# A two-layer expert stage: the second product in one pass of 512 columns, outputs in rows of 4 KB

## The chip, the cores and the metric

The kernel runs on one core of one Trainium2 chip. The metric is the device time of one execution in microseconds; the median of several executions is compared. The profile comes from one execution, which has its own time.

The core has a matrix engine (TensorE, PE in the profile, with PEld for its weight loads), VectorE (DVE), ScalarE (ACT), GpSimd (POOL) and a queue, SP, which issues all transfers of this kernel. TensorE reads SBUF and writes PSUM; ScalarE and VectorE copy from PSUM to SBUF. Transfers between SBUF and device memory run on 16 DMA engines.

## The reference

Three stages in a row on 2304 tokens of 512 features (4 sequences of 576).

```python
x = attention(q, k, v)                      # 8 heads of 64; 4 local, 4 strided masks
h = x @ w_in                                # 512 -> 2048
x = (h * sigmoid(1.702 * h)) @ w_out        # 2048 -> 512
logits = x @ phi                            # 32 slots: 8 experts of 4
slot_input = softmax_over_tokens(logits).T @ x
for e in range(8):                          # 4 slots of each expert
    slot_out[e] = relu(slot_input[e] @ w1[e]) @ w2[e]   # 512 -> 1024 -> 512
out = softmax_over_slots(logits) @ slot_out # (2304, 32) @ (32, 512)
```

The output is 2304 x 512 in float32, 4.72 MB. The weights w1 and w2 of the experts are 16.8 MB each.

## The kernel before

Most of the span is attention and the 512 to 2048 product, with the token softmax gathered on the way. The change touches only the last part, the experts and the output.

All 32 slots of the 8 experts go through TensorE at once. The 128 rows of a weight tile are 128 values of the inner dimension; a tile of 1 MB holds [128, 4, 512] floats. `load_ex` (L479) asks SP for the next tile; `ex[0]` to `ex[3]` are parts of w_out, `ex[4]` to `ex[19]` belong to the first expert product, `ex[20]` to `ex[35]` to the second. They go into buffers that other work has freed: `e`, `x0`, `x1` and `wi` tiles, and parts of the large tile gT, which `gx_tile` (L474) hands out as four slots of [128, 4, 512] in turn. A load waits on SP until the last user of its buffer is done. Tiles 23 to 35 take buffers of first-product tiles (or of others freed then), and so are issued as that product goes on.

The slot inputs are made at L590 to L598: spp is summed on TensorE, copied to `acc_s` in two halves (VectorE L592, ScalarE L593), multiplied with a selection (sip) and copied to `si`. `expand1(G, n)` (L632) makes the first product for four experts and half of the hidden units: 16 matmuls of 512 columns into one PSUM tile hp. `hidden_t` turns it for the second product.

`expand2(half, n)` (L658, matmul at L667) is the second product. The 512 output columns are cut into blocks of 256, 128 and 128:

```python
COLS = [(0, 256), (256, 128), (384, 128)]
```

On the host (`_layouts`), w2 is laid out so that a tile of 1 MB holds 2 (or 4) of the 16 slices of the inner dimension for the columns of one block, with 4 experts beside one another. So the first block uses tiles 20 to 27, the second 28 to 31, the third 32 to 35. A float32 matmul has two records in the profile. `slot_out(half)` (L669) takes a finished block from PSUM: ScalarE writes one part of `so` (L672), VectorE the other (L673).

The combine weights of the tokens, one number for each token and slot, are split in two parts (`combine_split`, L609), turned by TensorE and copied by ScalarE into cT (`combine_t`, L619, copy at L624), five chunks of 512 tokens (the last of 256). The order of instructions on an engine is set by a planner that follows the program's order by priority and the estimated readiness; in the profile, three of the five L624 copies stand at 386 to 389 us.

`combine(half, k, n)` (L675) makes the output for n groups of 128 tokens and one block of columns: a matmul for each group (L684), copies to one of the four slots of gT, by ScalarE (L687) and VectorE (L689) in turn, and one store (L690). A partition holds one token of each group, so a row of the store is the block's width: 1 KB or 512 B. Blocks 0 and 1 are combined between the `expand2` calls of the following block, the last one at the end:

```python
for half in range(1, len(COLS)):
    todo = list(PARTS)
    tiles = COLS[half][1] // 32
    for n in range(tiles):
        expand2(half, n)
        if n:
            for _ in range(-(-len(todo) // (tiles - n))):
                combine(half - 1, *todo.pop(0))
    slot_out(half)
```

Two other lines serve below for comparison: L241, where ScalarE writes attention outputs into x, contiguous for the local heads and with a step of 32 tokens for the strided ones, and the store of w_out slices to device memory (wo_scr), in rows of 2 KB. L319 is the product with w_in, in fp32r, the type of the combine matmul.

Of the kernel before, what the change touches and what calls it, by code (L numbers as in the profile page):

```python
# [9 lines left out]
F32 = mybir.dt.float32  # L10
# [4 lines left out]
ALU = mybir.AluOpType  # L15
# [4 lines left out]
NT, DM, FF = B * S, 512, 2048  # L20
# [9 lines left out]
CHUNKS = [(0, 512), (512, 512), (1024, 512), (1536, 512), (2048, 256)]  # L30
NF = FF // 128
TFROM = 5
COLS = [(0, 256), (256, 128), (384, 128)]
PARTS = [(0, 2), (2, 4), (6, 4), (10, 4), (14, 4)]
LAST = [(0, 4), (4, 4), (8, 4), (12, 4), (16, 2)]
F64_SMALL = float(np.uint32(897 << 20).view(np.float32))
F64_LARGE = float(np.uint32((1151 << 20) - 1).view(np.float32))
C_ID, C_REP, C_ZC, C_ML, C_ML0, C_MS, C_END = 0, 128, 256, 258, 354, 450, 514
# [3 lines left out]
def tile_kernel(ctx: ExitStack, tc: tile.TileContext, lqk, lv, sqk, sv, wraw, phi, wexp, cst, out):  # L42
    nc = tc.nc
    P = 128
# [4 lines left out]
    xp = ctx.enter_context(tc.tile_pool(name="xp", bufs=3))  # L49
# [15 lines left out]
    def mtile(name):  # L65
        return ps_m.tile([P, 512], F32, tag="m", name=name)
# [19 lines left out]
    zc = cs[:, C_ZC:C_ZC + 2]  # L86
# [263 lines left out]
    side, st, todo = [], {}, []  # L350
# [120 lines left out]
    ex = {}  # L471
    gxn = [0]

    def gx_tile():  # L474
        k = gxn[0] % 4
        gxn[0] += 1
        return gt[0][:, 4 * k:4 * k + 4]
# [95 lines left out]
    c = len(CHUNKS) - 1  # L573
# [14 lines left out]
    for f in range(NF):  # L588
        j = f % 4
# [10 lines left out]
    cT0 = tl.tile([P, 2048], F32R, name="cT0")  # L600
# [3 lines left out]
    def ttile(name):  # L604
        return ps_t.tile([P, 512], F32, tag="t", name=name)
# [3 lines left out]
    def combine_split(c):  # L609
        c0, N = CHUNKS[c]  # L610
        ntt = N // 128
        t = c4t[:, c % 2]
        c4s[c] = t
        c4 = t.rearrange("p (u r e q) -> p u r e q", r=2, e=2, q=8)[:, :4 * ntt]
        cc = ca[:, c0 // 128:c0 // 128 + ntt].rearrange("p t (j q) -> p (t j) q", q=8).unsqueeze(2).to_broadcast([P, 4 * ntt, 2, 8])
        nc.vector.tensor_copy(c4[:, :, :, 0].bitcast(F32R), cc)
        nc.vector.tensor_tensor(c4[:, :, :, 1].bitcast(F32R), cc, c4[:, :, :, 0], op=ALU.subtract)

    def combine_t(c):  # L619
        c0, N = CHUNKS[c]  # L620
        ctp = ttile(f"ctp_{c}")
        for tt in range(N // 128):
            nc.tensor.transpose(ctp[:, 128 * tt:128 * tt + 128], c4s[c][:, 128 * tt:128 * tt + 128], ident)
        nc.scalar.copy(cT0[:, c0:c0 + N] if c < 4 else cT1, ctp[:, :N])  # L624

    hzt = e1p.tile([P, 2, 8, P], F32, tag="e", name="hz")
    hc = e1p.tile([P, 4, 512], F32, tag="e", name="hc")
# [17 lines left out]
    def hidden_t(G, n):  # L645
        hT = mtile(f"hT_{G}_{n}")
        for q in range(4):
            nc.tensor.transpose(hT[:, 128 * q:128 * q + 128], h1[G, n][:, 128 * q:128 * q + 128], ident)
        sv = hT.rearrange("p (q m) -> p q m", m=128)
        dv = hz[G][:, 4 * n:4 * n + 4, :]  # L650
        for j in range(4):
            o = 40 * j + 4 * G
            nc.vector.tensor_copy(dv[:, :, 32 * j:32 * j + 32].rearrange("p f (r q) -> p f r q", q=8)[:, :, :, 4 * G:4 * G + 4],
                                  sv[:, :, o:o + 4].unsqueeze(2).to_broadcast([P, 4, 4, 4]))

    ops, obs = [], {}

    def expand2(half, n):  # L658
        c0, w = COLS[half]
        per = DM // w  # L660
        if n == 0:
            ops.append(mtile(f"op_{half}"))
        t = ex[20 + c0 // 32 + n].rearrange("p j f -> p (j f)").rearrange("p (k j f) -> p k j f", k=per, j=4)
        for k in range(per):
            G, fc = (per * n + k) // 8, (per * n + k) % 8
            for j in range(4):
                nc.tensor.matmul(ops[half][32 * j:32 * j + 32, :w], hz[G][:, fc, 32 * j:32 * j + 32], t[:, k, j], start=G + fc == 0, stop=G + fc == 8)  # L667

    def slot_out(half):  # L669
        c0, w = COLS[half]  # L670
        o = ops[half][:, :w]
        nc.scalar.mul(so[:, 0, c0:c0 + w], o, zc[:, 0:1])  # L672
        nc.vector.scalar_tensor_tensor(so[:, 1, c0:c0 + w], o, zc[:, 1:2], so[:, 0, c0:c0 + w].bitcast(F32), op0=ALU.mult, op1=ALU.add)  # L673

    def combine(half, k, n):  # L675
        c0, w = COLS[half]
        per = DM // w
        ob = gx_tile().rearrange("p a b -> p (a b)")[:, :n * w].rearrange("p (t f) -> p t f", f=w)
        for a in range(0, n, per):
            z = min(n, a + per)  # L680
            fp = ttile(f"fp_{half}_{k}_{a}")[:, :w * (z - a)].rearrange("p (t f) -> p t f", f=w)
            for t in range(a, z):
                tok = P * (k + t)
                nc.tensor.matmul(fp[:, t - a], cT0[:, tok:tok + P] if k + t < 16 else cT1[:, tok - 2048:tok - 2048 + P], so[:, 1, c0:c0 + w], start=True, stop=True)  # L684
            obs[0] = not obs.get(0)
            if obs[0]:
                nc.scalar.copy(ob[:, a:z], fp)  # L687
            else:
                nc.vector.tensor_copy(ob[:, a:z], fp)  # L689
        nc.sync.dma_start(out[P * k:P * (k + n), c0:c0 + w].rearrange("(t p) f -> p t f", p=P), ob)  # L690

    expand1(0, 0)
    hz = [hzt[:, 0], hzt[:, 1]]
# [11 lines left out]
    for c in range(2):  # L705
        combine_split(c)
        combine_t(c)
# [9 lines left out]
    fin = e1p.tile([P, 4, 512], F32R, tag="e", name="fin")  # L717
    so, cT1 = fin[:, :2], fin[:, 2, :256]
    hidden_t(1, 0)
    for n in range(8):  # L720
        expand2(0, n)
        if n == 2:
            hidden_t(1, 1)
        if n >= 5:
            combine_split(n - 3)
            combine_t(n - 3)
    slot_out(0)
    for half in range(1, len(COLS)):
        todo = list(PARTS)
        tiles = COLS[half][1] // 32  # L730
        for n in range(tiles):
            expand2(half, n)
            if n:
                for _ in range(-(-len(todo) // (tiles - n))):
                    combine(half - 1, *todo.pop(0))
        slot_out(half)
    for k, n in LAST:
        combine(len(COLS) - 1, k, n)


def _layouts(q, k, v, w_in, w_out, phi, w1, w2):
# [63 lines left out]
```

## Time and profile before

| | us |
|---|---|
| timed runs, median (lowest, highest) | 441.59 (441.43, 441.65) |
| profiled execution | 442.75 |
| its span (first to last instruction) | 441.0 |
| busy: TensorE / VectorE / ScalarE / GpSimd | 410.5 / 264.9 / 195.3 / 78.5 |
| DMA | 80.90 MB, mean 183 GB/s |

A line of the profile names the source line, engine and operation, the tile written and the tiles read, the shape and a count. Starts are counted from the span's start. In brackets stands how long the engine was idle before, and what released it. The granted clock is TensorE's: 1.00 is 2.4 GHz, 0.50 is 1.2 GHz. Busy time of a matmul includes its way through the pipeline, so neighbouring records overlap. DMA share is the mean busy share of the 16 DMA engines; packets may overlap, so it can pass 1.

### The profile page before, as it was taken

How to read it: one execution, taken by the hardware profiler on the slowest of the kernel's cores; microseconds unless marked ns; L12 is line 12 of the kernel's file. 1: busy time of each engine (PE TensorE's matmuls, PEld its weight loads, DVE VectorE, ACT ScalarE, POOL GpSimd, SP SyncE). 2: the span in 40 equal slices, each digit the busy share in tenths (PEclk: the TensorE clock that was granted, in tenths of full speed). 3: DMA queues.
4: the chain of work that ended last, by engine and by line, in shares of the span. 5: the costliest groups of instructions: out<-in, count | busy, mean ns of one | idle time of the engine just before them, and what ended most of it. 6: DMA issues, size and time to landing. Idle time of an engine off the chain costs nothing.

```text
span 441.0 us, 10075 instructions
## 1 busy us (share of the span) xinstructions
PE 410.5 (93%) x4082; PEld 282.8 (64%) x4088; DVE 264.9 (60%) x564; ACT 195.3 (44%) x639; POOL 78.5 (18%) x96
## 2 busy tenths in 40 slices
PE   8877898998989999999999999999999998999965
PEld 4555675655556767777676776776777795244654
DVE  2689999998987454565466535546454654431212
ACT  2785777766674644454543355321212222020312
POOL 0354445645540110100100001000000000000000
PEclk9999999999999999999999999999999999899995
DMA  8956757585663030221411101870003799779998
GB/s 245 358 164 221 248 177 278 182 310 180 223 199 113 9 100 2 91 81 52 153 42 58 38 2 36 283 289 1 1 0 143 291 387 349 271 305 424 426 355 251
DMA packets 25614, 80.90 MB, mean 183 GB/s; under 512 B 2144, under 2 KB 9440, under 8 KB 21472
## 3 DMA queue, kind: packets, MB, share of 16 engines
q1 hardware_dynamic: 25568, 80.26, 51.3%
q8 instruction: 32, 0.52, 0.5%
q14 instruction: 14, 0.11, 0.1%
HBM read 71.34 MB, written 8.91 MB: 182 GB/s over the span
## 4 chain that ended last, share of the span: by engine, by line
PE 67%; DVE 15%; ACT 6%; DMA 4%; POOL 4%; issue 3%; ACTq 0%; POOLq 0%
PE h L319 37%; PE u L433 5%; DMA out<-gT 4%; DVE wc L262 4%; PE lg L338 4%; PE s L161 3%; PE hp L637 3%; ACT ts L179 3%; DVE wc L263 3%; PE op L667 2%; PE ptp L197 2%; DVE wc L261 2%; PE av L216 2%; POOL wc L260 2%; PE busy L78 2%
## 5 line engine op out<-in xcount | busy, mean ns | idle before, releaser
L319 PE MATMUL h<-x,wi 128*128 128x512 f32 (+1 forms) x960 | 222.3, 379 | 1.2 <-DVE x L242 1.1
L319 PEld LDWEIGHTS h<-x,wi 128*128 128x128 f32 x960 | 161.8, 189 | 47.1 <-issue 13.8
L323 DVE SCALAR_TENSOR_TENSOR gT<-gT,h 128x512 f32<-128x512 f32 (+1 forms) x64 | 40.6, 634 | 62.2 <-ACT gT L322 61.6
L322 ACT ACTIVATE gT<-h 128x512 f32<-128x512 f32 (+1 forms) x64 | 35.5, 555 | 69.3 <-PE h L319 69.0
L179 ACT ACTIVATE ts<-ts,nmx 128x64 f32<-128x64 f32 (+1 forms) x120 | 41.6, 348 | 29.2 <-DVE nmx L174 28.9
L182 POOL TENSOR_TENSOR ts<-ts,sm 128x384 f32<-128x384 f32 (+2 forms) x32 | 28.6, 894 | 138.9 <-DVE sm L181 74.9
L346 DVE STREAM_TRANSPOSE gT<-gT 128x512 f32<-128x512 f32 (+1 forms) x64 | 41.0, 648 | 0.8
L260 POOL TENSOR_SCALAR wc<-wc 128x512 f32<-128x512 f32 x32 | 24.2, 759 | 29.1 <-ACT wc L259 29.1
L262 DVE SCALAR_TENSOR_TENSOR wc<-raw,wc 128x512 uint32<-128x512 uint32 x32 | 26.8, 839 | 0.3
L263 DVE SCALAR_TENSOR_TENSOR wc<-raw,wc 128x512 uint32<-128x512 uint32 x32 | 26.7, 835 | 0.2
L338 PE MATMUL lg<-gT,wp 128*32 128x512 f32 (+1 forms) x128 | 25.6, 564 | 0.7 <-ACT wp L295 0.6
L271 POOL TENSOR_TENSOR wi<-wc,wi 128x512 fp32r<-128x512 f32 x16 | 23.0, 1436 | 14.1 <-ACT wi L270 14.1
L197 PE MATMUL ptp<-cs,ts 128*96 128x128 f32 (+1 forms) x120 | 17.7, 280 | 8.4 <-POOL ts L182 7.7
L161 PE MATMUL s<-qk 64*64 64x96 f32 (+1 forms) x552 | 25.0, 236 | 0.2 <-DMA qk<-lqk 0.2
L161 PEld LDWEIGHTS s<-qk 64*64 64x64 f32 x552 | 20.9, 134 | 6.4 <-issue 4.9
L180 DVE TENSOR_SCALAR sm<-sm 128x5 f32<-128x5 f32 (+2 forms) x32 | 8.6, 268 | 26.7 <-ACT ts L179 26.7
L241 ACT CAST x<-av 128x320 fp32r<-128x320 f32 (+20 forms) x54 | 19.0, 396 | 10.8 <-DVE x L242 8.8
L197 PEld LDWEIGHTS ptp<-cs,ts 128*96 128x96 f32 (+1 forms) x120 | 12.8, 132 | 16.8 <-POOL ts L182 13.6
L433 PE MATMUL u<-gT,dT 32*32 32x512 f32 x576 | 21.5, 639 | 2.1 <-DVE z L408 2.1
L201 ACT COPY pt<-ptp 96x384 f32<-96x384 f32 (+1 forms) x34 | 14.9, 482 | 18.8 <-PE ptp L197 18.8
L261 DVE TENSOR_SCALAR wc<-wc 128x512 uint32<-128x512 uint32 x32 | 18.6, 584 | 7.2 <-POOL wc L260 7.1
L179 ACT ACTIVATION_READ_ACCUMULATOR ts<-ts,nmx 128x1 f32 x120 | 22.5, 187 | 0.0
(123 smaller groups left out, 467.8 us busy)
## 6 DMA issues: line engine op xcount, KB each, us to landing
ex<-wexp SPq DMA_DIRECT2D x28, 1024.0 KB, 7.8
raw<-wraw SPq DMA_DIRECT2D x32, 512.0 KB, 3.8
qk<-lqk SPq DMA_DIRECT2D x8, 592.0 KB, 4.8
wo_scr<-wc SPq DMA_DIRECT2D x16, 256.0 KB, 2.2
ex<-wo_scr SPq DMA_DIRECT2D x4, 1024.0 KB, 9.2
gT<-wexp SPq DMA_DIRECT2D x4, 1024.0 KB, 5.9
qk<-sqk SPq DMA_DIRECT2D x6, 604.0 KB, 4.2
v<-lv SPq DMA_DIRECT2D x8, 432.0 KB, 4.4
```

Of the source, the lines that this page charges most:

```text
L161: nc.tensor.matmul(sp[hs, u], t[hs, qo:qo + 64], t[hs, ko + qo:ko + qo + nk], start=not early, stop=not early or u == nt - 1)
L179: nc.scalar.activation(ts[:, u], src[:, u], AF.Exp, scale=sc, bias=nmx[:, u:u + 1], accum_out=sm[:, u:u + 1])
L197: nc.tensor.transpose(ptp[:nk, u - a], src, ident)
L260: nc.gpsimd.tensor_scalar(t, t, F64_LARGE, F64_SMALL, op0=ALU.min, op1=ALU.max)
L262: nc.vector.scalar_tensor_tensor(u, raw[:, :, 1], 0xC0000000, u, op0=ALU.bitwise_and, op1=ALU.bitwise_or)
L263: nc.vector.scalar_tensor_tensor(u, raw[:, :, 0], 29, u, op0=ALU.logical_shift_right, op1=ALU.bitwise_or)
L319: nc.tensor.matmul(h[:, :N], w[:, we, 128 * kt:128 * kt + 128], x[xe][:, kt, :N], start=n == 0, stop=n == 11)
L322: nc.scalar.activation(g[:, :N], h[:, :N], AF.Tanh, scale=0.851)
L323: nc.vector.scalar_tensor_tensor(g[:, :N], g[:, :N], 1.0, h[:, :N], op0=ALU.add, op1=ALU.mult)
L338: nc.tensor.matmul(lgs[c][32 * j:32 * j + 32, :N], wp[:, f0 + j, :], gs[c, f0 + j][:, :N], start=f0 == 0, stop=f0 == NF - 4)
L346: nc.vector.transpose(t_slots(c)[:, f, :N], gs[c, f][:, :N])
L433: nc.tensor.matmul(us[a][32 * j:32 * j + 32, :].rearrange("p (t f) -> p t f", f=32), dT[q, 32 * b:32 * b + 32], gT[q, :, 32 * b:32 * b + 3 ...
```

## The change

The second product is made in one pass over all 512 columns. With `COLS = [(0, 512)]` the host lays out w2 so that each of the 16 tiles is one slice of the inner dimension, with 4 experts of 512 columns; `expand2(n)` has four matmuls of 512 columns. All of w2 has to be there before the first output is ready. `slot_out` follows once, in two halves of 256 columns. Then all of `combine` comes, chunk by chunk.

A partition now holds four consecutive tokens (two in the last chunk). To that end `combine_t` writes cT with the tokens sorted anew, so that ScalarE's writes lie 128 elements apart. Two tokens of all 512 columns are stored together: nine stores of 512 KB, a row of which is 4 KB in one piece. The output buffers are the four slots of gT and one `x0` tile; none is used twice. The splits and transposes of chunks 2 to 4 move from after tiles 5, 6 and 7 of the old first block to after tiles 5, 7 and 9.

```diff
@@ -30,9 +30,7 @@
 CHUNKS = [(0, 512), (512, 512), (1024, 512), (1536, 512), (2048, 256)]
 NF = FF // 128
 TFROM = 5
-COLS = [(0, 256), (256, 128), (384, 128)]
-PARTS = [(0, 2), (2, 4), (6, 4), (10, 4), (14, 4)]
-LAST = [(0, 4), (4, 4), (8, 4), (12, 4), (16, 2)]
+COLS = [(0, 512)]
 F64_SMALL = float(np.uint32(897 << 20).view(np.float32))
 F64_LARGE = float(np.uint32((1151 << 20) - 1).view(np.float32))
 C_ID, C_REP, C_ZC, C_ML, C_ML0, C_MS, C_END = 0, 128, 256, 258, 354, 450, 514
@@ -621,7 +619,8 @@
         ctp = ttile(f"ctp_{c}")
         for tt in range(N // 128):
             nc.tensor.transpose(ctp[:, 128 * tt:128 * tt + 128], c4s[c][:, 128 * tt:128 * tt + 128], ident)
-        nc.scalar.copy(cT0[:, c0:c0 + N] if c < 4 else cT1, ctp[:, :N])
+        t = cT0[:, c0:c0 + N] if c < 4 else cT1
+        nc.scalar.copy(t.rearrange("k (t p) -> k p t", p=P), ctp[:, :N].rearrange("k (p t) -> k p t", p=P))
 
     hzt = e1p.tile([P, 2, 8, P], F32, tag="e", name="hz")
     hc = e1p.tile([P, 4, 512], F32, tag="e", name="hc")
@@ -653,41 +652,33 @@
             nc.vector.tensor_copy(dv[:, :, 32 * j:32 * j + 32].rearrange("p f (r q) -> p f r q", q=8)[:, :, :, 4 * G:4 * G + 4],
                                   sv[:, :, o:o + 4].unsqueeze(2).to_broadcast([P, 4, 4, 4]))
 
-    ops, obs = [], {}
-
-    def expand2(half, n):
-        c0, w = COLS[half]
-        per = DM // w
+    op = []
+
+    def expand2(n):
         if n == 0:
-            ops.append(mtile(f"op_{half}"))
-        t = ex[20 + c0 // 32 + n].rearrange("p j f -> p (j f)").rearrange("p (k j f) -> p k j f", k=per, j=4)
-        for k in range(per):
-            G, fc = (per * n + k) // 8, (per * n + k) % 8
-            for j in range(4):
-                nc.tensor.matmul(ops[half][32 * j:32 * j + 32, :w], hz[G][:, fc, 32 * j:32 * j + 32], t[:, k, j], start=G + fc == 0, stop=G + fc == 8)
-
-    def slot_out(half):
-        c0, w = COLS[half]
-        o = ops[half][:, :w]
-        nc.scalar.mul(so[:, 0, c0:c0 + w], o, zc[:, 0:1])
-        nc.vector.scalar_tensor_tensor(so[:, 1, c0:c0 + w], o, zc[:, 1:2], so[:, 0, c0:c0 + w].bitcast(F32), op0=ALU.mult, op1=ALU.add)
-
-    def combine(half, k, n):
-        c0, w = COLS[half]
-        per = DM // w
-        ob = gx_tile().rearrange("p a b -> p (a b)")[:, :n * w].rearrange("p (t f) -> p t f", f=w)
-        for a in range(0, n, per):
-            z = min(n, a + per)
-            fp = ttile(f"fp_{half}_{k}_{a}")[:, :w * (z - a)].rearrange("p (t f) -> p t f", f=w)
-            for t in range(a, z):
-                tok = P * (k + t)
-                nc.tensor.matmul(fp[:, t - a], cT0[:, tok:tok + P] if k + t < 16 else cT1[:, tok - 2048:tok - 2048 + P], so[:, 1, c0:c0 + w], start=True, stop=True)
-            obs[0] = not obs.get(0)
-            if obs[0]:
-                nc.scalar.copy(ob[:, a:z], fp)
-            else:
-                nc.vector.tensor_copy(ob[:, a:z], fp)
-        nc.sync.dma_start(out[P * k:P * (k + n), c0:c0 + w].rearrange("(t p) f -> p t f", p=P), ob)
+            op.append(mtile("op"))
+        G, fc = n // 8, n % 8
+        for j in range(4):
+            nc.tensor.matmul(op[0][32 * j:32 * j + 32, :], hz[G][:, fc, 32 * j:32 * j + 32], ex[20 + n][:, j, :], start=n == 0, stop=n == 15)
+
+    def slot_out():
+        for c0 in (0, 256):
+            o = op[0][:, c0:c0 + 256]
+            nc.scalar.mul(so[:, 0, c0:c0 + 256], o, zc[:, 0:1])
+            nc.vector.scalar_tensor_tensor(so[:, 1, c0:c0 + 256], o, zc[:, 1:2], so[:, 0, c0:c0 + 256].bitcast(F32), op0=ALU.mult, op1=ALU.add)
+
+    def combine(c):
+        c0, N = CHUNKS[c]
+        ntt = N // 128
+        ob = gx_tile() if c < 4 else xp.tile([P, 2, 512], F32, tag="x0", name="ob_last")
+        dst = out[c0:c0 + N].rearrange("(p t) f -> p t f", t=ntt)
+        for t in range(ntt):
+            fp = (ttile if t % 2 else mtile)(f"fp_{c}_{t}")
+            w = cT0[:, c0 + P * t:c0 + P * t + P] if c < 4 else cT1[:, P * t:P * t + P]
+            nc.tensor.matmul(fp, w, so[:, 1], start=True, stop=True)
+            (nc.vector.tensor_copy if t % 2 else nc.scalar.copy)(ob[:, t], fp)
+            if t % 2:
+                nc.sync.dma_start(dst[:, t - 1:t + 1], ob[:, t - 1:t + 1])
 
     expand1(0, 0)
     hz = [hzt[:, 0], hzt[:, 1]]
@@ -717,25 +708,17 @@
     fin = e1p.tile([P, 4, 512], F32R, tag="e", name="fin")
     so, cT1 = fin[:, :2], fin[:, 2, :256]
     hidden_t(1, 0)
-    for n in range(8):
-        expand2(0, n)
+    for n in range(NF):
+        expand2(n)
         if n == 2:
             hidden_t(1, 1)
-        if n >= 5:
-            combine_split(n - 3)
-            combine_t(n - 3)
-    slot_out(0)
-    for half in range(1, len(COLS)):
-        todo = list(PARTS)
-        tiles = COLS[half][1] // 32
-        for n in range(tiles):
-            expand2(half, n)
-            if n:
-                for _ in range(-(-len(todo) // (tiles - n))):
-                    combine(half - 1, *todo.pop(0))
-        slot_out(half)
-    for k, n in LAST:
-        combine(len(COLS) - 1, k, n)
+        if n in (5, 7, 9):
+            c = (n - 1) // 2
+            combine_split(c)
+            combine_t(c)
+    slot_out()
+    for c in range(len(CHUNKS)):
+        combine(c)
 
 
 def _layouts(q, k, v, w_in, w_out, phi, w1, w2):
```

## Rows read from the trace of the kernel before

**Rows 1.** Page, moved GB/s in 40 slices of the span (each 11 us)

```profile
GB/s 245 358 164 221 248 177 278 182 310 180 223 199 113 9 100 2 91 81 52 153 42 58 38 2 36 283 289 1 1 0 143 291 387 349 271 305 424 426 355 251
```

**Rows 2.** Windows (us; busy us by engine, granted clock, DMA share, GB/s)

```profile
391.00:421.00 30.00, 28.82 (x402) 14.67 (x394) 6.47 (x23) 5.71 (x11) 0.00 (x0) 1.00 1.00 418
421.00:427.00 6.00, 3.78 (x110) 3.44 (x114) 0.00 (x0) 0.00 (x0) 0.00 (x0) 1.00 1.01 338
431.00:435.00 4.00, 3.50 (x14) 3.12 (x15) 1.42 (x3) 1.17 (x2) 0.00 (x0) 0.50 0.66 201
435.00:439.00 4.00, 1.94 (x10) 1.75 (x9) 1.35 (x2) 0.96 (x2) 0.00 (x0) 0.50 1.15 345
373.00:375.00 2.00, 0.00 (x0) 0.00 (x0) 1.04 (x6) 1.03 (x5) 0.00 (x0) 0.93 0.94 381
375.00:378.00 3.00, 2.97 (x60) 1.09 (x64) 0.94 (x8) 0.00 (x0) 0.00 (x0) 0.50 0.59 246
427.00:429.30 2.30, 1.55 (x36) 1.14 (x28) 1.37 (x3) 0.37 (x1) 0.00 (x0) 1.00 0.95 329
```

**Rows 3.** Waits of the DMA queue SP, 383 to 392 us: total, times, longest

```profile
SPq L485 <- PE hp L637: 7.0, 3, 6.2
```

**Rows 4.** DMA issues at 402.18, 404.79, 437.90: size, us to landing

```profile
ex<-wexp SPq DMA_DIRECT2D x1, 1024.0 KB, 20.8
ex<-wexp SPq DMA_DIRECT2D x1, 1024.0 KB, 22.0
out<-gT SPq DMA_DIRECT2D x1, 128.0 KB, 2.1
```

**Rows 5.** Timeline, 402 to 442 us (start, us; in brackets idle before and its releaser)

```profile
402.18 0.33 SPq L485 DMA_DIRECT2D ex<-wexp  x1
404.79 0.33 SPq L485 DMA_DIRECT2D ex<-wexp  x1
412.65 0.47 ACT L672 ACTIVATE fin<-op,cs 128x256 fp32r<-128x256 f32 x1 [0.44 <-PE op L667]
413.16 0.48 DVE L673 SCALAR_TENSOR_TENSOR fin<-op,cs,fin 128x256 fp32r<-128x256 f32 x1 [4.77 <-ACT fin L672]
426.81 1.08 PE L667 MATMUL op<-ex,hz 128*32 128x128 f32 x32 [2.22 <-DMA ex<-wexp]
427.61 0.69 DVE L689 COPY gT<-fp 128x512 f32<-128x512 f32 x1 [6.71 <-DMA out<-gT]
```

**Rows 6.** The line of the output stores: ns min/median/max, first and last start

```profile
L690 SPq DMA_DIRECT2D out<-gT x15: 372/373/3867, 415.9 to 437.9; - x15
```

**Rows 7.** Chain that ended last, 404 to 442 us (start, us, what)

```profile
418.07 12.17 DMA out<-gT
```

**Rows 8.** Timeline, 380 to 397 us, around the slot inputs

```profile
386.18 0.59 ACT L624 CAST cT<-ctp 128x512 fp32r<-128x512 f32 x1 [6.38 <-issue]
386.66 0.38 ACT L593 COPY acc_s<-spp 128x256 f32<-128x256 f32 x1
394.47 1.04 PE L637 MATMUL hp<-gT,si 128*32 128x512 f32 x8
```

**Rows 9.** Groups by line and shape: busy us, mean ns

```profile
L624 ACT CAST cT<-ctp 128x512 fp32r<-128x512 f32 x4 | 2.3, 586 | 18.1 <-PE ctp L623 11.7 <-issue 6.4
L241 ACT CAST x<-av 128x320 fp32r<-128x320 f32 x8 | 3.4, 422 | 0.8 <-PE av L216 0.6
L241 ACT CAST x<-av 128x288 fp32r<-128x288 f32 x2 | 1.4, 724 | 0.0
```

**Rows 10.** Page, the costliest group: TensorE's fp32r products of 512 columns

```profile
L319 PE MATMUL h<-x,wi 128*128 128x512 f32 (+1 forms) x960 | 222.3, 379 | 1.2 <-DVE x L242 1.1
```

**Rows 11.** DMA packets, 415 to 427 us

```profile
DMA packets 1479, 4.60 MB, mean 384 GB/s; under 512 B 93, under 2 KB 1036, under 8 KB 1036
```

**Rows 12.** DMA, 134.5 to 137 us, the last store to wo_scr (slices of 62.5 ns)

```profile
GB/s 0 148 0 0 0 0 0 0 0 0 0 0 0 0 0 0 0 0 262 459 393 328 360 459 393 295 426 459 230 131 0 0 0 0 0 0 0 0 0 0
wo_scr<-wc SPq DMA_DIRECT2D x1, 256.0 KB, 2.0
```

## The prediction

> **What bounds the kernel now.** I read the page's slices first, then the windows of the last 50 us, the waits of the DMA queue, the DMA issues, the timeline and the chain of waits. From 391 us the moved GB/s stand at their ceiling [rows 1]: 30 us at 418 GB/s with the DMA engines busy all the time [rows 2]. These are the 1 MB expert tiles. They are asked for as the first expert product frees their buffers: SP waits 7.0 us on it between 383 and 392 [rows 3]. The last two tiles land 20.8 and 22.0 us after their issues [rows 4] at 402.18 and 404.79 [rows 5], so at 423.0 and 426.8; TensorE's last product in op starts at 426.81, released by that DMA [rows 5]. Up to 426.8 the transfers set the time and TensorE follows.
>
> The tail of 14.2 us behind that is already half done inside the transfers. Blocks of 256 and 128 columns are finished while later tiles are on the way, and their 15 stores are issued from 415.9 to 437.9 [rows 6]. They queue behind the loads: one of 418.07 lands 12.17 us later, and this piece stands in the chain [rows 7]. From 431 to 435 the DMA engines are only 0.66 busy, at 201 GB/s [rows 2], because copies wait for the four store buffers, VectorE once for 6.71 us [rows 5]; then rows of 512 B flow at 345 GB/s [rows 2]. The last store lands 2.1 us after its issue [rows 4], at 440.0, and the span ends 1.0 us later.
>
> **The change part by part.** All times are on the clock of the profiled execution: span 441.0, whole run 442.75; the median of the timed runs is 441.59. A difference in span is added to the median.
>
> Second product. Before, it is 64 products of 256 columns and 128 of 128; now 64 of 512. That is the same 32,768 columns, and all but the last tile lies under the loads. One tile is 4 matmuls (8 records), 1.04 us in the first product's rows of the same shape [rows 8], at 2.4 GHz. A tile arrives every 2.51 us (1.049 MB at 418 GB/s), so TensorE, which starts when several tiles are there, catches up with them and then waits for each.
>
> Last tile. No store is queued among the loads any more. The tile before the last lands at 423.0; one more at 418 GB/s is 425.5, where it was 426.8. From 421 to 427 the rate was 338 GB/s [rows 2], with about 1000 packets of the stores among the rest [rows 11], so I give the 1.3 us to the stores and take 425.5; the other end is 426.8, no gain.
>
> Strided copies in combine_t. ScalarE now writes cT with its four tokens 512 B apart. Contiguous, 512 columns take 586 ns; the nearest strided row is 724 ns for 288 columns, against 422 for 320 contiguous ones [rows 9]. That grows to some 1.2 us for 512. The last two of the five have room: ScalarE waits for op then, and nothing needs them before 428. The first three stand at 386 to 389, and half of acc_s is copied behind the first of them (386.18, then 386.66 [rows 8]). With 0.6 us more, less what TensorE was busy with anyway, the slot inputs come some 0.5 us later. That isn't hidden, since the loads wait there for the first product [rows 3]: the whole stream moves. I take +0.5; the ends are 0 (another order on ScalarE) and +1.2 (two copies ahead of it). The last tile lands at 426.0.
>
> Last product. That is 1.04 us at 2.4 GHz. The granted clock fell to 0.50 at 375, after 2 us without a matmul, and again behind 429.3, after TensorE had waited for the last tile and for copies [rows 2]. In the changed kernel it works 1.04 us of every 2.51 for the last ten microseconds of loads, so I take 1.2 GHz: 2.08 us and 0.05 to start, to 428.1. The other end is 1.04.
>
> slot_out began at 412.65 for the first block [rows 5]; now all of it stands behind the last tile, in two halves: 0.07 to start, ScalarE 0.47, VectorE 0.48 twice [rows 5], 0.05 between them; ScalarE's second half lies beside VectorE's first. That makes 1.55, to 429.65.
>
> First outputs. 18 matmuls of 512 columns replace 54, at 0.23 us each at 2.4 GHz (222.3 us for 960 [rows 10]) and 0.46 at 1.2. The first store needs two of them and a VectorE copy of 0.69 [rows 5]: 0.05 + 0.92 + 0.1 + 0.69 + 0.05 is 1.8 (1.4 at 2.4 GHz), so its issue is at 431.45. After that a pair costs at most 0.92 us on TensorE and 0.7 on each copying engine, below the 1.31 us that a store of 512 KB takes at 400 GB/s: the stores hide the rest. Nine issues replace fifteen, and no copy waits for a buffer, since each chunk has its own.
>
> Stores. All 4.72 MB now leave behind the loads; before, 1036 packets of at most 1 KB, about 1 MB, had left by 427 [rows 11]. The rates of stores: 345 GB/s for 512 B rows [rows 2]; the last store of wo_scr, of 2 KB rows, has slices from 262 to 459, some 380 in the mean of its ten full ones [rows 12]; loads of 8 KB rows have 418. For 4 KB rows I take 400, between the two nearest: 11.8 us. The ends are 13.7 (345) and 11.1 (424, a little over the loads' mean). For issue and landing around the data: that store of wo_scr took 2.0 us for 0.26 MB [rows 12], 0.65 of it data, so 1.4. Together 13.2, to 444.65, and 1.0 to the end as now.
>
> **Sum.** 425.5 + 0.5 + 2.1 + 1.55 + 1.8 + 13.2 + 1.0 = 445.65, which is 4.65 us above 441.0: 441.59 + 4.65 = 446.2 us. From the last tile to the end it took 14.2 us and will take 19.65. The narrow rows and the stalls that go are worth some 4 us, but 1 MB more is exposed (2.5 us), and the last product, slot_out, the first outputs and the first store's start, 6.9 us, lie between loads and stores with the DMA engines empty.
>
> **Rivals.**
> - The clock stays at 2.4 GHz. For it: it was still 1.00 from 427 to 429.3 [rows 2], after a wait. Then 1.04 and 0.4 us go: 444.8. Against it: ten microseconds of short products.
> - Stores are bound near 345 GB/s whatever their rows. For it: the 512 B stores run there with a DMA share of 1.15 [rows 2], so something may be full. Against it: the slices above 390 of wo_scr. 13.7 in place of 11.8: 448.1. The Trainium skill, DMA: Bandwidth & Descriptors, section "Where 436 GB/s comes from", says that between HBM and SBUF the HBM side binds, at about 358 GB/s for a core; by that figure the stores would take an estimated 13.2 us and the run 447.6. The loads of this trace, 418 GB/s over 30 us [rows 2], stand against it, and for wide stores no run here shows it yet.
> - The slow end of the loads was not the stores' doing: 426.8 stays, and the time is 447.5. For it: the tile before the last still landed on pace, at 423.0, so the stores had little of the loads left to hold up.
> - The wide rows don't reach the wire: each is cut into two pieces of 2 KB. 380 GB/s, 12.4 us, 446.8.
> - The other side, not slower: the stores took far more from the last loads than I think. At 415 some 443 packets of 8 KB (1479 less 1036) were left [rows 11], 3.6 MB; shared evenly at 424 GB/s they end at 423.6. With the clock at 2.4 GHz, strided copies that cost nothing and stores at 424: 423.6 + 1.1 + 1.55 + 1.4 + 12.5 + 1.0 = 441.15, or 441.7 as a median, no change. It becomes faster only if the last tile lands before about 422.6, and against that the tile before it landed at 423.0.
>
> **How the numbers follow.** Forecast 0.47, clock 0.13, stores at 345 0.15, slow end 0.09, pieces of 2 KB 0.07, other side 0.09. The range reaches from the clock rival with stores at 424 and strided copies that are hidden (444.8 less 0.7 and 0.5) at 443.6 to the stores' rival with half of the slow end, 448.8. No change means within 0.2% (0.9 us), about what can be told apart: only the other side reaches it, 0.05, or goes beyond it, 0.04; all else is slower, 0.91.
>
> **What would show it.** Right: no store before 430; DMA engines empty for some 7 us between the last tile (425.5 to 427) and the first store's data; op's last tiles each released by a DMA; a granted clock of 0.50 in the stores; nine stores of 512 KB that land about 1.3 us apart. Wrong: stores that land closer than 1.1 us apart, a last tile before 423, or copies that wait for a store's buffer.

## The result, and the profile after

The changed kernel is slower: a median of 446.66 us (446.05 to 447.45, 5 runs) against 441.65 (441.43 to 444.64, 5 runs), a ratio of 1.0096 (95% interval 1.0073 to 1.0118). Its profiled execution took 446.90 us, its span is 445.1; before these were 442.75 and 441.0.

The page's slices (span; granted clock in tenths; GB/s, here 11.1 us each):

```profile
span 445.1 us, 9472 instructions
PEclk9999999999999999999999999999999998999957
GB/s 248 349 162 219 246 187 264 194 301 189 225 180 115 1 98 9 83 91 52 141 88 11 38 38 7 376 185 1 0 0 214 328 357 331 286 339 426 427 92 369
```

Up to the third slice from the end it is the picture of before [rows 1]. Then comes a slice of 92 GB/s that was not there. The windows show the same more sharply (busy by engine, clock, DMA share, GB/s):

```profile
391.00:421.00 30.00, 27.47 (x239) 8.24 (x235) 3.67 (x18) 2.91 (x4) 0.00 (x0) 1.00 1.00 417
425.60:432.40 6.80, 4.56 (x15) 2.28 (x16) 2.28 (x4) 2.32 (x5) 0.00 (x0) 0.50 0.00 0
433.00:443.00 10.00, 2.98 (x12) 1.97 (x10) 4.15 (x7) 3.13 (x6) 0.00 (x0) 0.84 1.03 421
```

The loads run at 417 GB/s as before [rows 2]. Then the DMA engines move nothing for some 7 us: the first store is issued at 431.7, and its data move from 432.5 on. Then come 421 GB/s of stores without a pause. TensorE works in the empty stretch, at a granted clock of 0.50; during the stores it is 0.84.

The issues of the last two tiles, of the first store and of the last (size, us to landing):

```profile
ex<-wexp SPq DMA_DIRECT2D x1, 1024.0 KB, 20.3
ex<-wexp SPq DMA_DIRECT2D x1, 1024.0 KB, 19.9
out<-gT SPq DMA_DIRECT2D x1, 512.0 KB, 2.7
out<-ob_last SPq DMA_DIRECT2D x1, 512.0 KB, 4.8
```

Their times and what lies between them are in the timeline:

```profile
405.57 0.33 SPq L483 DMA_DIRECT2D ex<-wexp  x1
423.04 1.77 PE L662 MATMUL op<-ex,hz 128*32 128x512 f32 x8 [1.35 <-DMA ex<-wexp]
425.52 1.94 PE L662 MATMUL op<-ex,hz 128*32 128x512 f32 x8 [0.72 <-DMA ex<-wexp]
427.53 0.47 ACT L667 ACTIVATE fin<-op,cs 128x256 fp32r<-128x256 f32 x1 [11.70 <-PE op L662]
428.04 0.48 DVE L668 SCALAR_TENSOR_TENSOR fin<-op,cs,fin 128x256 fp32r<-128x256 f32 x1 [19.12 <-ACT fin L667]
428.56 0.48 ACT L667 ACTIVATE fin<-op,cs 128x256 fp32r<-128x256 f32 x1 [0.55 <-DVE fin L668]
429.07 0.48 DVE L668 SCALAR_TENSOR_TENSOR fin<-op,cs,fin 128x256 fp32r<-128x256 f32 x1 [0.55 <-ACT fin L667]
429.70 5.23 PE L678 MATMUL fp<-fin,cT 128*128 128x512 f32 x14 [2.24 <-DVE fin L668]
430.92 0.69 DVE L679 COPY gT<-fp 128x512 f32<-128x512 f32 x1 [1.37 <-PE fp L678]
431.68 7.66 SPq L681 DMA_DIRECT2D out<-gT  x8
439.44 1.12 SPq L681 DMA_DIRECT2D out<-ob_last  x1
```

The last two tiles, issued at 402.71 and 405.57, land at 423.0 and 425.5 (before: 423.0 and 426.8 [rows 4, 5]). From there one thing follows another: the last product, 425.52 to 427.50; slot_out, four instructions, to 429.55; two output matmuls and a copy, first store issued at 431.68; last store issued at 439.44, landed at 444.25. From the last tile to the last landing it is 18.8 us, where it was 13.2. This tail is 5.5 us longer (before rounding), the last tile lands 1.3 us earlier, and what follows the last landing is 0.1 shorter: together the 4.1 us by which the span grew.

The stretch of the slot inputs, to be held against [rows 8]:

```profile
386.49 1.08 ACT L623 CAST cT<-ctp 128x512 fp32r<-128x512 f32 x1 [6.38 <-issue]
387.36 0.43 ACT L591 COPY acc_s<-spp 128x256 f32<-128x256 f32 x1
388.98 6.21 PE L636 MATMUL hp<-ex,si 128*32 128x512 f32 x56
```

ScalarE's cT copy takes 1.08 us with its strided writes, so acc_s is copied at 387.36 and the first product begins at 388.98 (before: 388.44). Counted from the start of spp (381.87 before, 382.19 now) that is 6.79 us in place of 6.57.

### The profile page after: what moved, and what is told of

It is laid out like the page before. It is cut to its first block, busy times and chain, and to the rows that moved or that the text cites. A ratio compares the mean times of both kernels' runs of the same rounds, so it can differ in the third digit from the quotient of the medians.

```text
span 445.1 us, 9472 instructions
## 1 busy us (share of the span) xinstructions
PE 408.6 (92%) x3796; PEld 270.7 (61%) x3796; DVE 264.7 (59%) x563; ACT 196.7 (44%) x637; POOL 78.4 (18%) x96
## 4 chain that ended last, share of the span: by engine, by line
PE 60%; DVE 16%; DMA 8%; ACT 6%; issue 4%; POOL 4%; DVEq 0%; POOLq 0%; ACTq 0%; SPq 0%
PE h L317 37%; DMA ex<-wexp 7%; PE u L431 5%; DVE wc L260 4%; PE lg L336 4%; PE s L159 3%; ACT ts L177 3%; DVE wc L261 3%; PE ptp L195 2%; DVE wc L259 2%; PE av L214 2%; PE busy L76 2%; POOL wc L258 2%; POOL ts L180 1%; DVE nmx L172 1%
## 5 line engine op out<-in xcount | busy, mean ns | idle before, releaser
L199 ACT COPY pt<-ptp 96x384 f32<-96x384 f32 (+1 forms) x34 | 15.0, 482 | 18.8 <-PE ptp L195 18.8
```

## The experiments

One caution ahead: beside the experiments the kernel before had medians of 442.6 and 442.5 us in place of 441.65, with single runs from 440.9 to 444.6, so a time that was expected in microseconds is to be held against the measured one by way of the ratio. In the profiled executions the last tile lands anywhere from 423.7 to 428.9, because the stages ahead of it vary (the product of the slot inputs, spp, starts at 380.2 in e3_slot and at 385.5 in e1_rows2k). Medians tell the whole effect; the single steps I read within each trace, from the landing of the last tile on. "Last two tiles" is the time between their landings, each worked out as issue plus time to landing; "tail" goes from the landing of the last tile to that of the last store, worked out likewise.

| kernel | last two tiles, us | tail, us | ratio to before (95%) |
|---|---|---|---|
| before | 3.8 | 13.2 | |
| changed | 2.5 | 18.8 | 1.0096 (1.0073 to 1.0118) |
| e1_rows2k | 2.6 | 19.2 | 1.0095 (1.0058 to 1.0131) |
| e2_warm | 2.6 | 19.1 | 1.0083 (1.0059 to 1.0108) |
| e6_warm2 | 2.6 | 17.4 | 1.0085 (1.0058 to 1.0111) |
| e3_slot | 2.6 | 18.2 | 1.0091 (1.0065 to 1.0118) |
| e8_both | 2.4 | 16.8 | 1.0061 (1.0039 to 1.0084) |
| e4_bufs | 3.9 | 13.0 | 0.9998 (0.9983 to 1.0014) |
| e5_two | 4.3 | 12.4 | 0.9976 (0.9959 to 0.9993) |
| e7_two_warm | 4.2 | 12.3 | 0.9970 (0.9953 to 0.9986) |

**The rows and the copies alone: e1_rows2k.**

```diff
-        nc.scalar.copy(t.rearrange("k (t p) -> k p t", p=P), ctp[:, :N].rearrange("k (p t) -> k p t", p=P))
+        nc.scalar.copy(t, ctp[:, :N])
...
-        dst = out[c0:c0 + N].rearrange("(p t) f -> p t f", t=ntt)
+        dst = out[c0:c0 + N].rearrange("(t p) f -> p t f", p=P)
```

> The changed kernel with the tokens as before: one token per partition and group, stores in rows of 2 KB, cT copied contiguously. The product still runs in one pass. Theory (the place of the stores costs the time: all 4.72 MB and the chain from the last tile to the first store lie behind the loads): it stays slow. Rows of 2 KB at 380 to 400 GB/s in place of 421 add 0.6 to 1.2 us, contiguous copies give 0.2 back: 447.0 to 447.7 us against 446.7 of the changed kernel. Rival (the sorted tokens, with strided copies and wide rows, are what costs): it comes back to 441.6 to 443.

It stays slow, so the sorted tokens are not the cause. The extra 0.3 to 1.0 us that was expected on top doesn't show in the ratio, 1.0095 beside 1.0096, whose interval is wider than that; what the narrower rows cost is read from the trace. The store stretch (slices of 0.375 us, packets):

```profile
GB/s 0 0 153 410 410 393 410 415 399 410 415 399 410 415 399 410 415 399 410 404 404 415 421 382 421 421 382 421 415 399 410 415 399 208 0 0 0 0 0 0
DMA packets 2448, 4.72 MB, mean 315 GB/s; under 512 B 144, under 2 KB 144, under 8 KB 2448
```

and that of the changed kernel:

```profile
DMA packets 1296, 4.72 MB, mean 328 GB/s; under 512 B 144, under 2 KB 144, under 8 KB 1296
```

Less 144 short ones, the same 4.72 MB need 2304 packets of 2 KB instead of 1152 of 4 KB, and some 408 GB/s (512 KB in 1.285 us from one landing to the next) instead of 423 (1.239). Wider rows are worth 0.4 us of the tail here. The contiguous copies give the 0.2 us at the slot inputs back: from spp to the first product it is 6.56 us.

**TensorE kept busy: e2_warm, then e6_warm2.** Behind each of the tiles 30 to 35, dummy matmuls on that tile:

```diff
+        if n >= 10:
+            bz = ttile(f"bz_{n}")
+            for _ in range(3):      # e6_warm2: 2
+                nc.tensor.matmul(bz[:, :256], ident, ex[20 + n][:, 0, :256], start=True, stop=True)
```

> The changed kernel with three more float32 matmuls of 256 columns behind each of the tiles 30 to 35, into a PSUM tile that nobody reads, so that TensorE does not idle while it waits for tiles. Theory: the granted clock stays at 1.00 through the last product and the first outputs, the last product takes 1.05 us in place of 1.98 and the first store is issued 0.4 earlier on top: 1.2 to 1.4 us less, 445.3 to 445.5. Rival (the clock is the main loss): 443.5 or less. Third: the extra matmuls delay the product and nothing is won, 446.7 or more.

The ratio, 1.0083, rules out the rival (443.5 or less, a ratio of 1.004) but can't tell the theory from no gain, since its interval holds the 1.0096 of the changed kernel too. In the trace the third case came: the product is delayed, and the tail is 19.1 us, no shorter than 18.8. Timeline of e2_warm:

```profile
425.56 1.06 PE L662 MATMUL op<-ex,hz 128*32 128x512 f32 x8
426.56 1.56 PE L666 MATMUL bz<-ex,cs 128*128 128x256 f32 x6
428.05 1.06 PE L662 MATMUL op<-ex,hz 128*32 128x512 f32 x8
432.78 7.58 SPq L685 DMA_DIRECT2D out<-gT  x8
```

Product and dummies together take 2.49 us for a tile (425.56 to 428.05), and tiles come every 2.43; with a backlog at the start, TensorE never catches up. The last tile had landed at 426.3 (405.88 and 20.4), and its product starts at 428.05. From there to the first store it is 4.73 us in place of 6.16, as the theory has it; 1.74 us of lateness eat that.

> As e2_warm, but two extra matmuls of 256 columns behind each of the tiles 30 to 35, 1.0 us in place of 1.5, so that TensorE is done with them before the next tile lands. Theory: the last product starts when the last tile lands (within 0.1 us), takes 1.05 us at 2.4 GHz, and from its start to the first store pass 4.7 us, as in e2_warm, in place of 6.16: 1.4 us less than the changed kernel, a ratio to the kernel before of 1.006 to 1.007. Rival (the clock is the main loss): 1.003 or less.

```profile
426.15 1.06 PE L662 MATMUL op<-ex,hz 128*32 128x512 f32 x8 [0.44 <-DMA ex<-wexp]
430.89 7.63 SPq L685 DMA_DIRECT2D out<-gT  x8
```

```profile
424.00:431.00 7.00, 5.48 (x31) 2.88 (x24) 1.83 (x4) 2.05 (x5) 0.00 (x0) 1.00 0.03 13
```

Now the product starts with the landing (426.1), the clock stays at 1.00, and the first store is issued 4.74 us later. The tail is 1.4 us shorter than in the changed kernel, the size expected. The median ratio (1.0085) moved by less than expected and its interval (1.0058 to 1.0111) holds both, though not the rival's 1.003; the step is shown in the trace, its whole worth in runs is not.

**slot_out undivided: e3_slot.**

```diff
-        for c0 in (0, 256):
-            ...
+        nc.scalar.mul(so[:, 0], op[0], zc[:, 0:1])
+        nc.vector.scalar_tensor_tensor(so[:, 1], op[0], zc[:, 1:2], so[:, 0].bitcast(F32), op0=ALU.mult, op1=ALU.add)
```

> The changed kernel with slot_out in one ScalarE and one VectorE instruction of 512 columns in place of two halves each. In the changed kernel ScalarE's second half began only when VectorE's first had ended, and the four took 2.05 us. Theory (the two halves run one after the other, so halving wins nothing): 0.07 + 0.6 + 0.05 + 0.69, 1.4 us, 0.65 less; ratio to before 1.008. Rival (the halves overlap in part, one long pair is slower): 2.0 us or more between the product's end and the first output matmul.

```profile
423.75 1.93 PE L662 MATMUL op<-ex,hz 128*32 128x512 f32 x8 [0.72 <-DMA ex<-wexp]
425.75 0.69 ACT L665 ACTIVATE fin<-op,cs 128x512 fp32r<-128x512 f32 x1 [11.94 <-PE op L662]
426.47 0.75 DVE L666 SCALAR_TENSOR_TENSOR fin<-op,cs,fin 128x512 fp32r<-128x512 f32 x1 [19.58 <-ACT fin L665]
427.27 5.35 PE L676 MATMUL fp<-fin,cT 128*128 128x512 f32 x14 [1.59 <-DVE fin L666]
429.29 7.67 SPq L679 DMA_DIRECT2D out<-gT  x8
```

From the start of ScalarE to the first output matmul it is 1.52 us; in the changed kernel it was 2.17 (427.53 to 429.70). That is 0.65 less, and the tail is 0.6 shorter. The ratio, 1.0091 where 1.008 was expected, is too coarse to show it. The halves of the changed kernel stood in a row: ScalarE's second waited 0.55 us for VectorE's first.

**Both: e8_both** has the dummies of e6_warm2 and the slot_out of e3_slot.

> The single pass with the extra matmuls of e6_warm2 and the undivided slot_out of e3_slot. Theory: the two gains add, 2.0 us less than the changed kernel, a ratio to the kernel before of 1.004 to 1.006, still slower, because 4.72 MB of stores behind the loads (11.2 us at 421 GB/s) and some 5.4 us with the DMA engines empty remain. Rival (the single pass is at fault only through its chain): 1.000 or less.

The tail is 16.8 us, 2.0 less than in the changed kernel: the gains add. At 1.0061 (1.0039 to 1.0084) it is still slower than the kernel before, so the chain alone is not at fault: 4.72 MB behind the last tile remain.

**The tail of the kernel before: e4_bufs** gives each output its own place, by a counter in place of `gx_tile()`:

```diff
-        ob = gx_tile().rearrange("p a b -> p (a b)")[:, :n * w].rearrange("p (t f) -> p t f", f=w)
+        ob = out_buffer(n * w).rearrange("p (t f) -> p t f", f=w)
```

> The kernel before (blocks of 256, 128 and 128 columns) with a place of its own for each output: the 16 slices of gT in a row and one x0 tile, instead of four slots in turn. Theory (before, the tail behind the loads holds 2 to 2.5 us in which the DMA engines wait for copies that wait for buffers): stores flow without a pause from the last tile on, 3.75 MB at 347 GB/s and 1.4 and 1.0 around them, 439.0 to 440.0 us. Rival (narrow rows set the tail, the waits only stand beside it): 441.4 to 441.8, no change.

It won nothing, and my account of the tail before falls with it. Windows of e4_bufs:

```profile
431.00:435.00 4.00, 0.30 (x2) 0.16 (x2) 0.69 (x1) 0.52 (x2) 0.00 (x0) 0.92 1.05 320
435.00:438.00 3.00, 0.00 (x0) 0.00 (x0) 0.00 (x0) 0.00 (x0) 0.00 (x0) 0.50 1.06 318
438.00:441.00 3.00, 0.00 (x0) 0.00 (x0) 0.00 (x0) 0.00 (x0) 0.00 (x0) 0.50 0.12 36
```

and the share of its DMA engines from 436 to 441 us, in tenths (slices of 0.125 us):

```profile
DMA  9999999999999533333322211111100000000000
```

The pause of before (201 GB/s, share 0.66, from 431 to 435 [rows 2]) is filled. But in the last 3 us only 0.12 of the DMA engines' time is used, where the kernel before still moved stores at full pace up to 439 [rows 2]. The share falls in steps, to 0.5, 0.3, 0.2 and 0.1 over two microseconds: a few engines end later than the others. The completion marks agree with that reading; the trace has sixteen of them for each transfer, as many as there are DMA engines. Of the last store of e4_bufs, eleven marks come from 437.95 to 438.12 and the other five from 438.63 to 439.98. In the kernel before, all sixteen marks of the last store lie within 0.18 us (439.83 to 440.01). This lag comes out of the loads: the marks of the last tile lie 2.7 us apart in both kernels. In the kernel before it is 2.0 us for the store that lands at 433.3, 0.4 for the one at 434.9 and 0.2 to 0.3 from then on, so the laggards catch up in the pause; in e4_bufs it stays at 2.0 or more to the end. The trace doesn't name the engines, and why some lag is open. What is shown: filling the pause doesn't bring the end nearer.

**Two blocks: e5_two**, on top of e4_bufs:

```diff
-COLS = [(0, 256), (256, 128), (384, 128)]
+COLS = [(0, 256), (256, 256)]
...
-LAST = [(0, 4), (4, 4), (8, 4), (12, 4), (16, 2)]
+LAST = PARTS
```

> Two blocks of 256 columns, each output in a place of its own, rows of 1 KB: the stores of the first block queue behind the loads and move while the last block is finished. Theory: the DMA engines never stand empty between loads and stores; 4.72 MB at some 350 GB/s from 425.5 on, 13.5 us and 1.0: 439.5 to 440.5. Rival (a last block twice as wide exposes its product, slot_out and first outputs as the single pass does): 442.5 or more.

```profile
427.00:431.00 4.00, 2.53 (x19) 1.20 (x20) 0.48 (x1) 0.47 (x1) 0.00 (x0) 0.50 0.98 345
431.00:433.00 2.00, 2.00 (x9) 1.77 (x9) 1.38 (x2) 0.78 (x2) 0.00 (x0) 0.50 0.24 87
433.00:439.00 6.00, 2.21 (x9) 1.76 (x8) 2.08 (x3) 1.57 (x3) 0.00 (x0) 0.50 1.05 372
```

This is the other way to fewer, wider blocks, and it is faster than both kernels: 0.9976 (0.9959 to 0.9993), a quarter of a per cent, and just short of what was expected (439.5 to 440.5 of 441.65 us is 0.995 to 0.997). The stores of the first block take up the time that the last product and slot_out need; 1 KB rows flow at 372 GB/s once the first block's are through, where 512 B rows had 345 [rows 2]. That the engines never stand empty did not come true: from 431 to 433 their share is 0.24.

**e7_two_warm** adds two dummies behind each of the tiles 30 to 35.

> e5_two (two blocks of 256 columns, own buffers) with two extra matmuls of 256 columns behind each of the tiles 30 to 35. In e5_two the DMA engines were only some 0.2 busy from 431 to 433.5, between the stores of the first block and those of the second, and the clock was 0.50 from 427 on. Theory: the first store of the second block is issued 1.2 to 1.6 us earlier after the last tile, the pause shrinks to under 1 us and the end comes 1.0 to 2.0 us earlier than in e5_two: a ratio to the kernel before of 0.993 to 0.996. Rival (a few slow DMA engines set the end, and pauses only let them catch up, as with e4_bufs): 0.997 to 0.999, no gain on e5_two.

```profile
425.50:429.00 3.50, 3.45 (x29) 2.05 (x28) 0.62 (x2) 0.47 (x1) 0.00 (x0) 1.00 1.04 368
429.00:431.00 2.00, 1.60 (x10) 1.13 (x9) 1.76 (x3) 1.43 (x3) 0.00 (x0) 1.00 0.52 184
431.00:437.00 6.00, 0.89 (x6) 0.63 (x5) 1.36 (x3) 0.92 (x2) 0.00 (x0) 0.91 1.03 365
```

The clock stays up and the pause is shorter, but the tail is 12.3 us against 12.4, and the ratio, 0.9970, can't be told from e5_two's. The rival's number came. The first store of the second block is issued 4.1 us after the last tile lands, where it was 4.6: 0.6 us earlier in place of 1.2 to 1.6, in part because TensorE was again behind (its last product starts at 426.13, 0.6 us after the landing). And these 0.6 us go to the lag at the end, as the rival has it: the sixteen completion marks of the last store lie 0.9 us apart (436.95 to 437.82), in e5_two 0.2.

**What slows the last tile: e9_side1k, e10_side8k, e11_sideload.** In the table, the last two tiles land 3.8 to 4.3 us apart where stores are queued behind the loads, 2.4 to 2.6 where none are. These three put 2 MB of side traffic behind the loads of the changed kernel:

```diff
+        if n == 9:
+            for e in range(2):
+                t = xp.tile([P, 4, 512], F32, tag=f"x{e}", name=f"side_{e}")
+                ...
+                nc.sync.dma_start(wo_scr[8 * e:8 * e + 8, :, :256].rearrange("t p d -> p t d"), t.rearrange("p a (b d) -> p (a b) d", d=256))
```

(e10: the same bytes in rows of 8 KB; e11: `nc.sync.dma_start(t..., wexp[e])`, a load.)

> The changed kernel, with two stores of 1 MB in rows of 1 KB from otherwise free buffers into scratch memory that nobody reads any more, issued when the fifth cT copy is done, some 9 us ahead of the last tile, as the kernel before had its first output stores queued. Theory (stores that wait behind the loads on the same DMA engines slow the end of the loads): the last tile lands 3.8 to 4.3 us behind the one before it, as in the four kernels with stores queued there, in place of 2.4 to 2.7. Rival (the late last tile comes from the column blocks' own order of work): 2.4 to 2.7.

> As e9_side1k, with rows of 8 KB on both sides. If it is the many short rows that slow the loads: 2.4 to 2.7 us between the last two tiles. If it is that stores follow loads at all: 3.8 to 4.3, as with rows of 1 KB.

> As e9_side1k, with two loads of 1 MB of w1 tiles into these buffers, which nobody reads, in place of the stores. If stores are what slows the last tile: 2.4 to 2.7 us between the last two tiles of w2. If anything queued behind it does: 3.5 or more. In no case do two MB more cost much at the end, since they fit in the 6 us in which the DMA engines are empty: within 1.5 us of the changed kernel.

TensorE's last two products wait for these tiles. In e9_side1k:

```profile
423.67 1.94 PE L662 MATMUL op<-ex,hz 128*32 128x512 f32 x8 [1.34 <-DMA ex<-wexp]
427.87 1.94 PE L662 MATMUL op<-ex,hz 128*32 128x512 f32 x8 [2.27 <-DMA ex<-wexp]
```

in e10_side8k:

```profile
422.51 1.93 PE L662 MATMUL op<-ex,hz 128*32 128x512 f32 x8 [1.33 <-DMA ex<-wexp]
426.88 1.93 PE L662 MATMUL op<-ex,hz 128*32 128x512 f32 x8 [2.43 <-DMA ex<-wexp]
```

and in e11_sideload:

```profile
423.67 1.62 PE L662 MATMUL op<-ex,hz 128*32 128x512 f32 x8 [0.59 <-DMA ex<-wexp]
426.24 1.06 PE L662 MATMUL op<-ex,hz 128*32 128x512 f32 x8 [0.94 <-DMA ex<-wexp]
```

4.2 us from tile to tile with stores of 1 KB rows behind, 4.4 with 8 KB rows, 2.6 with loads. So it is that stores follow, not how wide they are, nor that something follows at all. These are single runs (449.4, 448.4 and 446.9 us beside 443.6 of the kernel before), so the readings are those of one execution each. When the loads are held up can be seen in the packets, those of the kernel before from 421.5 to 423.5, of e9_side1k and of e11_sideload from 422.5 to 424.5:

```profile
DMA packets 76, 0.60 MB, mean 299 GB/s; under 512 B 3, under 2 KB 3, under 8 KB 3
DMA packets 65, 0.53 MB, mean 266 GB/s; under 512 B 1, under 2 KB 1, under 8 KB 1
DMA packets 111, 0.80 MB, mean 401 GB/s; under 512 B 14, under 2 KB 14, under 8 KB 14
```

The DMA engines are busy in all three (shares of 1.04, 0.97 and 0.98), and no packet of a store (512 B or 1 KB) is among them yet. So with stores queued behind, the load packets themselves become slower, some two microseconds ahead of the first store's packet; the stores' own packets take their share only after that. Why is open.

The stores themselves cost nothing more: the tail of e9_side1k is 18.8 us, as in the changed kernel. That of e11_sideload is 17.9, because its last product took 1.06 us and not 1.94: the granted clock was 0.94 from 424.5 to 427.5, with the same work on TensorE. So even in a single pass the last product doesn't meet the low clock in every execution.

## Why the prediction was right, step by step

446.2 us was forecast and 446.66 measured; the span should have risen by 4.65 us and rose by 4.1. The medians rose by 5.0 us; most of the difference is that the profiled execution of before took 442.75 us, 1.1 more than its median.

- Last tile: 425.5 from the loads' pace was right (425.48), and giving the 1.3 us of before to the queued stores was right; e9 to e11 show it, in one execution each. But it is not only their packets that take time from the loads, since the loads slow down before the first of them moves. The further 0.5 for strided copies was mis-sized: the copies did grow (1.08 us; some 1.2 were assumed) and moved the first product, but by 0.22 counted from spp. And the whole stream did not move with it: the last tile but one is issued 0.5 us later (402.71, before 402.18) and lands at 423.0 in both kernels.
- Last product: 2.08 forecast, 1.98 measured, at 0.50 of the clock. The clock rival falls for this execution (not for each, as e11_sideload shows); e6_warm2 shows what it would have been worth in the tail, 1.4 us (1.45 in the forecast).
- slot_out: 1.55 forecast, 2.05 measured. I let ScalarE's second half run beside VectorE's first; it waited for it. e3_slot has the price.
- First outputs: 1.8 forecast, 2.1 measured (429.55 to 431.68).
- Stores: 13.2 forecast, 12.6 measured (431.68 to 444.25). 4 KB rows flow at 421 GB/s and not at 400. That settles the rival of 345. The Trainium skill, DMA: Bandwidth & Descriptors, section "Where 436 GB/s comes from", has HBM bind at about 358 GB/s for a core; the stores of this trace don't agree, at 421 over ten microseconds. The packets of 4 KB show that the rows arrive in one piece, so that rival falls too.
- End: 1.0 forecast, 0.85 measured.

Errors of half a microsecond stand on both sides and nearly cancel, so that the total came this close is luck in part; the order of the steps and the size of each were right to 0.6 us. Of the signs, the empty 7 us, the releases by DMA and the stores 1.24 us apart came; a granted clock of 0.50 in the stores did not, it is 0.84 from 433 to 443. One of the reasons was wrong, though it is no term of the sum: "The narrow rows and the stalls that go are worth some 4 us". By e4_bufs the stall of before was worth nothing by itself. The sum was made from the flow of the stores in the changed kernel, so it didn't suffer.

The cause is the place of the stores. In the single pass they all lie behind the last tile, and so does the chain that makes the first of them; the DMA engines, which bound this stage, are empty for some 7 us. Most of them wait even longer: thirteen of the sixteen completion marks of the last tile come from 423.9 to 424.3, and TensorE waits for the last, at 425.5. Shortening the chain (e8_both) takes 2 us of it; using it for the stores of a first block (e5_two) takes all but some 2 us, at the price of 1 KB rows, and beats both kernels.

## What to carry to other kernels

Where transfers bound a stage, count the microseconds in which their engines are empty before counting bytes for each row: here 4 KB rows instead of 1 KB or less raised the rate from some 350 to 421 GB/s, worth 2.3 us for 4.72 MB at these rates, and the single pass that they needed opened a hole of 7. A block that is done early is cover for the chain of the last one; of one, two and three blocks, two did best here. And a pause in a flow of transfers is not yet a loss: fill it once and look at the end.

## What the runs showed of the hardware

- Loads that are followed by stores end later: 3.8 to 4.4 us between the last two tiles in six kernels with stores queued behind, 2.4 to 2.6 in six with nothing behind, whatever the stores' rows. With 2 MB of loads behind it was 2.6 (e9 to e11 in one execution each). The loads slow down to 266 to 299 GB/s some 2 us ahead of the first store's packet.
- The DMA engines don't end together: the sixteen completion marks of the last tile lie 1.6 us apart in the changed kernel and 2.7 in the kernel before. A flow of stores without a pause keeps this lag (2.0 us at the end of e4_bufs), a pause removes it (0.2 us in the kernel before).
- Rates of stores by row, from this core alone: 345 GB/s at 512 B [rows 2], 365 to 372 at 1 KB (e7_two_warm, e5_two), 408 at 2 KB, 421 at 4 KB.
- A ScalarE copy of 512 columns from PSUM with writes 512 B apart takes 1.08 us, contiguous 0.586 [rows 9].
- Dummy matmuls hold the clock at 1.00, but in the single pass they paid only where they ended before the tile they bridge to (tail 17.4 us); 2.49 us of work for each 2.43 us of transfer lost what the clock gave (19.1, without them 18.8).
